# The output weights of a linear-attention block from sixteen 32-column products, and the work around them reordered

## The chip, the cores and the metric

The kernel runs on one core of a Trainium2 chip. The metric is the device time of one execution in microseconds (us). TensorE (PE) multiplies matrices, VectorE (DVE), ScalarE (ACT) and GpSimd (POOL) work on elements, and SyncE (SP) issues most of the transfers. PSUM, into which TensorE writes, has eight banks here called 0 to 7.

## The reference

For a sequence of 2048 rows of 448 elements, a linear-attention block with 16 heads of 28, and a gated feed-forward block; `phi` is positive, so the attention needs no softmax.

```python
def _A_ref(x, wqkv, wo):
    qkv = (x @ wqkv).reshape(B, S, 3, H, Dh).transpose(2, 0, 3, 1, 4)
    q, k, v = qkv[0], qkv[1], qkv[2]
    phi = lambda t: jnp.where(t > 0, t + 1, jnp.exp(t)) + 1e-6
    pq, pk = phi(q), phi(k)
    kv = jnp.einsum("bhsd,bhse->bhde", pk, v)
    z = jnp.einsum("bhsd->bhd", pk)
    num = jnp.einsum("bhqd,bhde->bhqe", pq, kv)
    den = jnp.einsum("bhqd,bhd->bhq", pq, z)[..., None] + 1e-6
    o = num / den
    return o.transpose(0, 2, 1, 3).reshape(B, S, D) @ wo
def _B_ref(x, w_gate, w_up, w_down):
    g, u = x @ w_gate, x @ w_up
    return (_gelu(g) * u) @ w_down
h = x + _A_ref(_layernorm(x), A_wqkv, A_wo)
h2 = h + _B_ref(_layernorm(h), B_w_gate, B_w_up, B_w_down)
```

## The kernel before, in words

**Tiles and stages.** The rows are cut into 16 tiles of 128, tiles into 8 pairs. First stage: each tile is normalised and transposed, `k_t` and `q_t` are its projections (four products of 448 columns each, L469), ScalarE and VectorE turn them into `pk` and `pq`, and the `pt` products (L488) sum pk against the normalised rows over all tiles in four PSUM banks (`BK_PT`, 4 to 7). Bank 7 also holds z in its upper half.

**The middle.** When the last `pt` product is done, `z1` (ScalarE) and `z0` (VectorE) bring z onto all partitions (`zbc`), and `evpD_3`, `evpA_0`, `evpA_1`, `evpD_2` copy the four banks to `pt_sb`. `kv` (L527, sixteen products of 112 columns) multiplies them with the v weights, and `kvm` masks the result into a block-diagonal `kvz`. The `w2` products (L547) multiply `kvz` with `wo`: the rows of the result, 448, are the rows of a folded output weight. Each of four groups writes one bank, and `evwA_0`, `evwD_1`, `evwA_2`, `evwD_3` copy them to `w2`. `dws0` and `dws1` are transfers that give `w2s`, a copy of w2 with its partition halves exchanged. Meanwhile the first pair of tiles gets its denominators: `t1` (pq times zbc, tile 0 on VectorE, others on GpSimd), `dr` (sum over a head), `deA` (plus epsilon, ScalarE), `rd` (reciprocal), `pn` (pq times rd, into `pqn`). `tro` (L599) transposes pqn on TensorE into banks 6 and 7, `evo` copies it out, and `out1` (L617) multiplies it with w2. Later pairs have the same steps in pair-wide form (`cqP`, `aqP`, `drP`, `deP`, `rdP`, `pnP`), a transposing transfer `oT`, and products on partition halves (`outA`, `outB`, L627 and L628). The q products that are left over fill TensorE's time between these.

**The feed-forward stage.** The normalised rows (`nh`, `wrap`, `hT`) are multiplied by gate and up weights in pairs of products that use one half of the rows of the array each (`gu2` for chunks of two tiles, `gu4` for chunks of four, L731 and L733). ScalarE's `ge` applies gelu to the gate's bank, VectorE's `hm` multiplies with the up bank into `hh`, each in two halves of 256 columns. `down` (L697, L678 for the last two tiles) sums over `hh`, `fo` adds the residual, `do` writes the tile. The last tile's columns are done in two pieces, so that the first piece's write overlaps the second's products.

**What sets the order.** Every operation is added to a graph, with buffers that it reads and writes, from which its waits follow. Which operation stands where on its engine is written out by hand: `ORDERS` lists the numbers of the operations for PE, ACT, DVE, POOL and SP. `HOLD` only says which of an operation's waits is issued first.

```python
self.order = {e: [self.all[int(i)] for i in o.split()] for e, o in zip(ENGS, orders)}
...
for w in sorted(keep, key=lambda w: (w[4] not in hold, -w[1])):
    slots.setdefault(w[2], []).append((w[0], w[1], w[4]))
```

## Time and profile before

| | |
|---|---|
| time, median of 3 runs | 190.62 us (190.51, 190.62, 191.12) |
| span of the profiled execution | 188.3 us |
| PE busy | 184.3 us (98%), 1813 matmuls |
| DVE busy | 129.3 us (69%) |
| ACT busy | 76.5 us (41%) |
| POOL busy | 50.0 us (27%) |

The span runs from the first to the last profiled instruction of one execution; that execution's own time is not listed apart from the three runs, of which the median lies 2.3 us above the span. Rows of a timeline give start, length, engine, line, operation, output and inputs, shape (for TensorE first the part of the array, rows by columns) and count. A row that merges several instructions ends when the last of them ends. Matmuls overlap: one of 448 columns is listed with some 0.35 us, while the next one may start after half of that.

### The profile page before, as it was taken

The numbers are of one execution on the slowest core, as the hardware profiler recorded it, in microseconds if no ns is written. First come the engines' busy times: TensorE is split into PE (matmuls) and PEld (weight loads), VectorE is DVE, ScalarE is ACT, GpSimd is POOL, SyncE is SP. The second block draws the span as 40 slices with busy tenths as digits, with TensorE's granted clock in tenths as the row PEclk, the third lists the DMA queues.
The fourth block names the chain that finished last, engine by engine and source line by source line (L and its number), as shares of the span: only waits on it lengthen the run. The fifth ranks groups of instructions, "written<-read, shape, count | busy, mean of one in ns | idle before, by whom it ended". The sixth has DMA issues, their size and how long they took to land.

```text
span 188.3 us, 4459 instructions
## 1 busy us (share of the span) xinstructions
PE 184.3 (98%) x1813; PEld 109.2 (58%) x1813; DVE 129.3 (69%) x330; ACT 76.5 (41%) x220; POOL 50.0 (27%) x91
## 2 busy tenths in 40 slices
PE   7999999999999999999999999999999999999994
PEld 7545555555688788965554555555545545454554
DVE  4999959999899998786796762562645244335432
ACT  3878752799963231432234222321242222224100
POOL 6067910704505686033614000206100000000000
PEclk9999999999999999999999999999999999999999
DMA  5996458999393526820005720000096000002024
GB/s 169 387 231 88 96 104 194 218 222 174 65 320 64 95 52 116 84 52 0 0 3 98 144 54 0 0 3 2 3 135 111 3 0 24 3 0 98 3 79 140
DMA packets 35076, 17.11 MB, mean 91 GB/s; under 512 B 26864, under 2 KB 33648, under 8 KB 35056
## 3 DMA queue, kind: packets, MB, share of 16 engines
q1 hardware_dynamic: 34432, 16.32, 41.1%
q10 hardware_dynamic: 624, 0.52, 0.8%
q8 instruction: 14, 0.23, 0.5%
q14 instruction: 6, 0.05, 0.1%
HBM read 8.26 MB, written 1.84 MB: 54 GB/s over the span
## 4 chain that ended last, share of the span: by engine, by line
PE 94%; DVE 3%; DMA 1%; issue 0%
PE ps L733 38%; PE ps L697 19%; PE ps L469 12%; PE ps L731 9%; PE ps L488 6%; PE ps L627 3%; PE ps L678 3%; PE ps L628 2%; DMA x_sb<-in_A_x_dram 1%; DVE st L413 1%; PE ps L617 1%; PE ps L547 1%; PE ps L527 1%; PE ps L443 0%; PE ps L654 0%; DVE den L572 0%
## 5 line engine op out<-in xcount | busy, mean ns | idle before, releaser
L733 PE MATMUL ps<-hnT,wgu_sb 64*128 64x512 bf16 (+1 forms) x490 | 88.8, 333 | 0.0
L731 PE MATMUL ps<-hnT,wgu_sb 64*128 64x512 bf16 (+1 forms) x490 | 88.6, 333 | 0.0
L751 ACT ACTIVATE gl<-ps 128x256 bf16<-128x256 f32 x112 | 36.6, 383 | 85.3 <-PE ps L731 84.4
L753 DVE TENSOR_TENSOR hh<-ps,gl 128x256 bf16<-128x256 f32 x112 | 42.1, 416 | 41.4 <-ACT gl L751 41.3
L733 PEld LDWEIGHTS ps<-hnT,wgu_sb 64*128 64x128 bf16 x490 | 45.2, 94 | 32.9 <-DVE hh L753 3.4
L731 PEld LDWEIGHTS ps<-hnT,wgu_sb 64*128 64x128 bf16 x490 | 45.4, 94 | 2.5
L697 PE MATMUL ps<-wd_sb,hh 64*128 64x448 bf16 x392 | 41.5, 349 | 0.0
L697 PEld LDWEIGHTS ps<-wd_sb,hh 64*128 64x128 bf16 x392 | 23.2, 94 | 14.5
L469 PE MATMUL ps<-wqk_sb,xnT 128*128 128x448 bf16 x128 | 27.4, 353 | 0.0
L413 DVE BATCH_NORM_STATS2 st<-x_sb 128x6 f32<-128x448 bf16 x32 | 19.2, 612 | 1.8 <-DMA x_sb<-in_A_x_dram 1.7
L585 POOL TENSOR_TENSOR t<-pq,zbc 128x448 f32<-128x448 bf16 x12 | 12.3, 1042 | 23.7 <-DVE pq L583 22.0
L469 PEld LDWEIGHTS ps<-wqk_sb,xnT 128*128 128x128 bf16 x128 | 11.9, 98 | 11.4 <-DVE pk L482 0.8
L488 PE MATMUL ps<-pk,xnn 128*128 128x448 bf16 x64 | 13.9, 352 | 0.0
L627 PE MATMUL ps<-w,pqnT 64*128 64x448 bf16 x49 | 11.5, 349 | 0.1
L425 POOL TENSOR_SCALAR ln<-mv 128x2 f32<-128x2 f32 x7 | 2.0, 291 | 35.2 <-DVE mv L414 35.0
L480 ACT ACTIVATE e<-ps 128x448 bf16<-128x448 f32 x16 | 8.5, 539 | 5.6 <-PE ps L469 5.5
L628 PE MATMUL ps<-pt_sb,pqnT 64*128 64x448 bf16 x42 | 10.2, 350 | 0.0
L633 DVE TENSOR_TENSOR x_sb<-ps,x_sb 128x448 bf16<-128x448 f32 x16 | 9.6, 616 | 0.7 <-PE ps L628 0.6
L662 POOL TENSOR_SCALAR hn<-x_sb,nm,rs 128x448 bf16<-128x448 bf16 x14 | 9.9, 719 | 0.4
L482 DVE SCALAR_TENSOR_TENSOR pk<-ps,e 128x448 bf16<-128x448 f32 x16 | 9.8, 617 | 0.1
L488 PEld LDWEIGHTS ps<-pk,xnn 128*128 128x128 bf16 x64 | 6.3, 98 | 5.9 <-DVE pk L482 0.3
L453 POOL TENSOR_SCALAR xnn<-x_sb,nm,rs 128x448 bf16<-128x448 bf16 x12 | 8.9, 744 | 2.2 <-ACT rs L422 1.9
(85 smaller groups left out, 160.5 us busy)
## 6 DMA issues: line engine op xcount, KB each, us to landing
out_dram<-x_sb SPq DMA_DIRECT2D x15, 112.0 KB, 1.8
wd_sb<-in_B_w_down_dram SPq DMA_DIRECT2D x1, 1568.0 KB, 8.4
x_sb<-in_A_x_dram SPq DMA_DIRECT2D x3, 448.0 KB, 5.9
wgu_sb<-in_B_w_gate_dram SPq DMA_DIRECT2D x1, 896.0 KB, 12.1
wgu_sb<-in_B_w_up_dram SPq DMA_DIRECT2D x1, 896.0 KB, 16.5
wgu_sb<-in_B_w_gate_dram SPq DMA_DIRECT2D x1, 672.0 KB, 6.1
wgu_sb<-in_B_w_up_dram SPq DMA_DIRECT2D x1, 672.0 KB, 8.5
wo_sb<-in_A_wo_dram SPq DMA_DIRECT2D x1, 392.0 KB, 7.5
```

Of the source, the lines that this page charges most:

```text
L413: op("dve", lambda e: e.bn_stats(st[:, t, :], src_ap), [b_src], [b_st[t]], "bnst%s_%d" % (tag, t))
L469: ins = e.matmul(ps[:, bk, 0:D], xnT[:, t, k, :], wqk_sb[:, k, c0:c0 + D], start=(k == 0), stop=(k == 3))
L488: ins = e.matmul(ps[:, BK_PT[c], 0:D], xnn[:, t % XN_R, c * 128:(c + 1) * 128], pk[:, ip, :], start=(t == 0), stop=(t == T - 1))
L585: op("pool", lambda e, n=n: e.tensor_tensor(t1[:, n, :], pq[:, a + n, :], zbc[:, :], ALU.mult), [b_pq[a + n]] + b_z, [b_t1[n]], "t1p_%d" % ...
L627: e.matmul(ps[:, BK_OUT[0], 0:D], pqnT[ra, i2, sg // 2, :], w2[ra, sg // 2, :], start=(sg == 0), stop=(sg == 5))
L628: ins = e.matmul(ps[:, BK_OUT[1], 0:D], pqnT[rb, i2, 3 + (sg + 1) // 2, :], (w2 if sg == 6 else w2s)[rb, sg // 2, :], start=(sg == 0), sto ...
L662: op("pool", lambda e, t=t, sh=sh: e.tensor_scalar(hn[:, sh, 0:D], x_sb[:, t, :], nm2[:, t:t + 1], rs2[:, t:t + 1], ALU.add, ALU.mult), [b ...
L697: ins = e.matmul(ps[:, bko[half][n], 0:D], hh[rows, j, sl[n]], wd_sb[rows, j, :], start=(j == 0 and (half == 0 or p == 6)), stop=(j == NJ ...
L731: first = e.matmul(psG[:, jj * N:(jj + 1) * N], wgu_sb[A_, k, j * 128:(j + 1) * 128], hnT[A_, ka_, c0:c0 + N], start=(k == 0), stop=(k == ...
L733: ins = e.matmul(psU[:, jj * N:(jj + 1) * N], wgu_sb[B_, k, j * 128:(j + 1) * 128], hnT[B_, kb_, c0:c0 + N], start=(k == 0), stop=(k == NK ...
L751: G.add("act", lambda e, gi=gi, cs_=cs_, psG=psG: e.activation(gl[:, gi, cs_], psG[:, cs_], AF.Gelu_apprx_tanh), r=[b_ps[BK_G[i]]], w=[b_g ...
L753: op("dve", lambda e, dst=dst, srcU=srcU, srcL=srcL: e.tensor_tensor(dst, srcU, srcL, ALU.mult), [b_ps[BK_U[i]], b_glh], [b_ar[j_][t % HR] ...
```

## The change

- The sum for `w2` is cut into blocks of 32 rows of the result: sixteen products with 32 columns of `kvz` each, which write 32 partitions of a bank; two blocks straddle two groups of heads and have two products each. `kvd`, a copy of 64 columns that gave the last group a full width, goes; the last 64 rows of w2's fourth piece are zeroed at the start instead (`w2pad`), and the exchanged copy `w2s` has a fourth piece, so that `dws1` carries 64x1792 instead of 64x1344 elements.
- The first pair's denominators and transposes (`a2_den(0)`) stand ahead of w2 in the graph, as they use banks that w2 then takes.
- The second pair (tiles 2 and 3) has its VectorE steps pair-wide, as the later pairs had already. `t1p_3` also waits for the first pair's pqn.
- Epsilon is a 29th column of `t1`, written once at the start; `deA` and `deP` go.
- All three full copies of the PT banks are ScalarE's (`evpA_0` to `evpA_2`).
- In the chunks of two tiles `ge` and `hm` work on 512 columns in one operation.
- The last tile's pieces are 320 and 128 columns instead of 224 and 224.
- `ORDERS` is new, and `HOLD` has an entry for most operations.

TensorE between the last `pt` products (L488, L560) and the first pair's output products (L617, L692); L469 and L541 are q products, L527 and L650 kv, L547 and L668 w2, L599 and L625 the transposes. Before:

```order
L488 MATMUL ps<-pk,xnn 128x448 x20
L469 MATMUL ps<-wqk_sb,xnT 128x448 x8
L527 MATMUL ps<-pt_sb,wv_sb 112x112 x16
L469 MATMUL ps<-wqk_sb,xnT 128x448 x8
L547 MATMUL ps<-wo_sb,hh 128x448 x6
L469 MATMUL ps<-wqk_sb,xnT 128x448 x4
L547 MATMUL ps<-wo_sb,hh 128x448
L599 MATMUL ps<-ident,pqn 128x128 x8
L469 MATMUL ps<-wqk_sb,xnT 128x448 x4
L617 MATMUL ps<-w,pqnT 128x448 x8
```

And now:

```order
L560 MATMUL ps<-pk,xnn 128x448 x20
L541 MATMUL ps<-wqk_sb,xnT 128x448 x12
L650 MATMUL ps<-pt_sb,wv_sb 112x112 x16
L625 MATMUL ps<-ident,pqn 128x128 x8
L541 MATMUL ps<-wqk_sb,xnT 128x448 x4
L668 MATMUL ps<-wo_sb,hh 32x448 x16
L541 MATMUL ps<-wqk_sb,xnT 128x448 x8
L692 MATMUL ps<-w,pqnT 128x448 x8
```

Three q tiles instead of two stand ahead of kv, the transposes moved from behind w2 to directly behind kv, and all of w2 stands together behind one more q tile.

ScalarE from z1 (L514, L637) to the copies of w2 (L551, L674); L519 and L642 are copies of PT banks, L574 the epsilon, L496/L497 and L568/L569 exponential and relu of q, L602 and L628 evo. Before:

```order
L514 ACTIVATE zbc<-ps 64x448
L519 ACTIVATE pt_sb<-ps 128x448 x2
L574 ACTIVATE den<-den,eps_d 128x16
L496 ACTIVATE eq<-ps 128x448 x2
L497 ACTIVATE pq<-ps 128x448
L574 ACTIVATE den<-den,eps_d 128x16 x2
L496 ACTIVATE eq<-ps 128x448
L497 ACTIVATE pq<-ps 128x448
L574 ACTIVATE den<-den,eps_d 128x16
L497 ACTIVATE pq<-ps 128x448
L551 ACTIVATE w<-ps 128x448 x2
```

And now:

```order
L637 ACTIVATE zbc<-ps 64x448
L642 ACTIVATE pt_sb<-ps 128x448 x2
L568 ACTIVATE eq<-ps 128x448
L642 ACTIVATE pt_sb<-ps 128x448
L568 ACTIVATE eq<-ps 128x448
L569 ACTIVATE pq<-ps 128x448 x2
L628 ACTIVATE pqnT<-ps 128x512 x2
L568 ACTIVATE eq<-ps 128x448
L569 ACTIVATE pq<-ps 128x448
L674 ACTIVATE w<-ps 128x448 x2
```

The third copy of a PT bank stands behind one exponential, and evo moved from behind w2's copies to ahead of them.

VectorE in the same place, from the copy of the fourth PT bank (L516, L639) on: L515 and L638 are z0, L569 and L597 t1, L572 and L600 dr, L575 and L602 rd, L576 and L603 pn, L531 and L654 kvm, L553 and L676 copies of w2; L609, L610, L613, L615 and L616 are cqP, aqP, drP, rdP and pnP. Before:

```order
L515 COPY zbc<-zbc 64x448
L565 TENSOR_TENSOR pq<-pq,eq 128x448
L569 TENSOR_TENSOR t<-pq,zbc 128x448
L572 TENSOR_REDUCE den<-t 128x16
L521 CAST pt_sb<-ps 128x448
L575 RECIPROCAL rd<-den 128x16
L572 TENSOR_REDUCE den<-t 128x16 x2
L531 TENSOR_TENSOR hh<-ps,mask 112x4x112
L575 RECIPROCAL rd<-den 128x16
L536 COPY hh<-hh 112x64
L572 TENSOR_REDUCE den<-t 128x16
L575 RECIPROCAL rd<-den 128x16
```

And now:

```order
L600 TENSOR_REDUCE den<-t 128x16
L602 RECIPROCAL rd<-den 128x16
L603 TENSOR_TENSOR pqn<-pq,rd 128x448 x2
L654 TENSOR_TENSOR hh<-ps,mask 112x4x112
L609 TENSOR_SCALAR eq<-eq 128x896
L613 TENSOR_REDUCE den<-t 128x32
L676 CAST w<-ps 128x448
L610 TENSOR_TENSOR pq<-pq,eq 128x896
L615 RECIPROCAL rd<-den 128x32
L676 CAST w<-ps 64x448
L616 TENSOR_TENSOR pqn<-pq,rd 128x896
```

Both pqn of the first pair now stand ahead of kvm, the copy of a PT bank is gone, and the second pair's wide steps stand among the copies of w2.

The diff, cut to what the steps speak of:

```diff
 ORDERS = (
...
-    " 190 157 203 216 169 181 232 182 248 194 195 207 220 208 236 252 221 237 253 238 222 294 257 260 301 297 299"
+    " 191 158 204 217 170 182 233 183 249 195 208 196 209 221 237 253 222 238 254 239 223 258 295 311 309 264 319"
...
 HOLD = {
-    66: (36,), 141: (140,), 165: (164,), 214: (213,), 216: (215,), 323: (302,), 326: (324,), 431: (340,), 704:
...
+    21: (20,), 33: (32,), 35: (34,), 36: (35,), 38: (35,), 42: (41,), 44: (43,), 45: (44,), 47: (44,),
...
-        t1 = sb("t1", [128, 2, D], F32)
+        t1 = sb("t1", [128, 2, H, DH + 1], F32)
...
-        w2s = pt_sb[:, 0:3, :]
+        w2s = pt_sb
...
+        op("dve", lambda e: e.memset(w2[B_, 3, :], 0.0), [], [b_w2t], "w2pad")
...
-        op("pool", lambda e: e.memset(eps_d[:], EPS), [], [b_epsd], "epsd")
+        op("pool", lambda e: e.memset(t1[:, :, :, DH:DH + 1], EPS), [], [b_epsd], "epsd")
...
-            if c in (0, 1):
+            if c in (0, 1, 2):
                 op("act", lambda e, c=c: e.activation(pt_sb[:, c, :], ps[:, BK_PT[c], 0:D], AF.Identity), [b_ps[BK_PT[c]]], [b_pt[c]], "evpA_%d" % c)
...
-        op("dve", lambda e: e.tensor_copy(kvz[:, 4 * D:4 * D + 64], kvz[:, 4 * D - 64:4 * D]), [b_kvm], [b_kvd], "kvd")
+        a2_den(0)
...
-        for c in range(4):
-            def fw2(e, c=c):
-                gs = (c, c + 1) if c < 3 else (3,)
-                ins = None
-                for g in gs:
-                    ins = e.matmul(ps[:, BK_W2[c], 0:D], kvc(g, c), wo_sb[:, g, :], start=(g == gs[0]), stop=(g == gs[-1]))
-                return ins
+        for c, parts in enumerate((((0, 0), (1, 0), (2, 0), (3, 0), (3, 1)), ((0, 1), (1, 1), (2, 1), (3, 2)), ((0, 2), (1, 2), (2, 2), (3, 3), (2, 3)), ((0, 3), (1, 3)))):
+            def fw2(e, c=c, parts=parts):
+                ins = None
+                for i, (q, g) in enumerate(parts):
+                    ins = e.matmul(ps[32 * q:32 * q + 32, BK_W2[c], 0:D], kvc(g, c, q), wo_sb[:, g, :],
+                                   start=q not in [x[0] for x in parts[:i]], stop=q not in [x[0] for x in parts[i + 1:]])
+                return ins
...
-            dma("sp", w2s[to, :, :], w2[of, 0:3, :], [b_w2s[h]], "dws%d" % h, r=b_w2[0:3], after=xts[-1:])
+            dma("sp", w2s[to, 0:3 + h, :], w2[of, 0:3 + h, :], [b_w2s[h]], "dws%d" % h, r=b_w2[0:3 + h], after=xts[-1:])
...
-            if p < 2:
+            if p < 1:
...
-                    op("act", lambda e, i=i: e.activation(den[:, i, :], den[:, i, :], AF.Identity, bias=eps_d[:, 0:1]), [b_den[i], b_epsd], [b_den[i]], "deA_%d" % t)
...
-            parts = [(BK_L[t][0], 0, D)] if t < T - 1 else [(BK_L[t][0], 0, D // 2), (BK_L[t][1], D // 2, D)]
+            parts = [(BK_L[t][0], 0, D)] if t < T - 1 else [(BK_L[t][0], 0, 320), (BK_L[t][1], 320, D)]
...
-                for hh_ in range(2):
-                    cs_ = slice(hh_ * 256, (hh_ + 1) * 256)
+                for hh_ in range(2 if nj == 1 else 1):
+                    cs_ = slice(hh_ * 256, (hh_ + 1) * 256) if nj == 1 else slice(0, 512)
```

102 lines of the change are left out of this document (53 added, 49 removed), and 135 rows, old and new, of tables (HOLD, ORDERS).

## The prediction

> **What bounds the kernel now.** I read the page's busy rows and slices first, then the waits of TensorE, then the timelines of the middle (27 to 52 us) and of the end.
>
> ```profile
> span 188.3 us, 4459 instructions
> ...
> PE 184.3 (98%) x1813; PEld 109.2 (58%) x1813; DVE 129.3 (69%) x330; ACT 76.5 (41%) x220; POOL 50.0 (27%) x91
> ...
> PEclk9999999999999999999999999999999999999999
> ```
>
> TensorE (PE) is busy for 98% of the span at the full clock. Ends of matmuls are modelled, so that alone does not prove that it never waits; the list of its waits does more:
>
> ```profile
> PE ps L407 <- POOL eps_d L383: 1.0, 1, 1.0
> PE ps L443 <- DVE xnn L435: 0.4, 1, 0.4
> ```
>
> Both belong to the first six microseconds, which the change leaves alone. A short wait can still hide under a modelled end, so I also read intervals between starts. This is TensorE in the middle (start, length, line, shape, count):
>
> ```profile
> 30.45 3.95 PE L488 MATMUL ps<-pk,xnn 128*128 128x448 bf16 x20
> 34.23 1.68 PE L469 MATMUL ps<-wqk_sb,xnT 128*128 128x448 bf16 x8
> 35.96 1.03 PE L527 MATMUL ps<-pt_sb,wv_sb 128*112 128x112 bf16 x16
> 36.83 1.68 PE L469 MATMUL ps<-wqk_sb,xnT 128*128 128x448 bf16 x8
> 38.34 1.30 PE L547 MATMUL ps<-wo_sb,hh 112*128 112x448 bf16 x6
> 39.48 0.92 PE L469 MATMUL ps<-wqk_sb,xnT 128*128 128x448 bf16 x4
> 40.24 0.35 PE L547 MATMUL ps<-wo_sb,hh 112*128 112x448 bf16 x1
> 40.43 0.61 PE L599 MATMUL ps<-ident,pqn 128*128 128x128 bf16 x8
> ```
>
> From 30.45 to 34.23 twenty 448-column matmuls start: 0.189 us each. Eight from 36.83 to 38.34 give 0.189 again. But the eight from 34.23 should end at 34.23 + 8 x 0.189 = 35.74, and the kv products (L527) start at 35.96: a wait of 0.22. The chain of waits says for what:
>
> ```profile
> 35.38 0.54 DVE pt_sb L521
> ...
> 35.96 1.03 PE ps L527 x16
> ...
> 40.59 0.45 PE ps L599 x8
> ```
>
> It is evpD_2, VectorE's copy of one of the PT banks. Elsewhere the kernel is a stream of matmuls at their own rate. So a gain has to come from fewer matmul intervals, from this 0.22, or from the end after the last matmul. What VectorE (DVE), ScalarE (ACT) or GpSimd (POOL) save is worth nothing unless TensorE waited for it.
>
> **The change part by part.**
>
> *kv's wait.* Twelve q products now stand ahead of kv in place of eight: kv is due at 34.23 + 12 x 0.189 = 36.50. The three copies of the PT banks go to ScalarE, with eq_5 between the second and the third.
>
> ```profile
> 34.43 0.98 ACT L519 ACTIVATE pt_sb<-ps 128x448 bf16<-128x448 f32 x2 [1.16 <-PE ps L488]
> ...
> 35.62 0.96 ACT L496 ACTIVATE eq<-ps 128x448 bf16<-128x448 f32 x2
> ...
> 40.88 1.08 ACT L602 ACTIVATE pqnT<-ps 128x512 bf16<-128x512 bf16 x2
> ```
>
> Two such operations take 0.96 to 0.98 together, so the next one starts some 0.43 after one. The third copy is the fourth operation from 34.43: it starts at 35.72 and ends 0.54 later, at 36.26, which is 0.24 ahead of 36.50. The wait goes: **-0.22**. If ScalarE slips by more than 0.24, kv waits again for the excess.
>
> *The output weights.* Before, seven products (six and one) take seven intervals: 1.32. Now there are sixteen products of 32 columns, each onto 32 partitions; products on different quarters of the array may run together, those on the same quarter not. The order is w2_3, w2_0, w2_1, w2_2, and the quarters in that order are 0 1, 0 1 2 3 3, 0 1 2 3, 0 1 2 3 2. Issued in order, with a quarter taken up again when it is free, that fills five intervals: (0 1) (0 1 2 3) (3 0 1 2) (3 0 1 2) (3 2), or 5 x 0.189 = 0.95. No product of a quarter of the columns stands in this trace. The nearest rows are products that use half of the rows each:
>
> ```profile
> 48.30 0.33 PE L654 MATMUL ps<-ident,hn 128*128 128x128 bf16 x3
> 48.57 0.36 PE L627 MATMUL ps<-w,pqnT 64*128 64x448 bf16 x1
> 48.57 0.36 PE L628 MATMUL ps<-pt_sb,pqnT 64*128 64x448 bf16 x1
> ...
> 180.08 0.35 PE L697 MATMUL ps<-wd_sb,hh 64*128 64x448 bf16 x1
> 180.36 0.36 PE L678 MATMUL ps<-wd_sb,hh 128*128 128x448 bf16 x1
> ```
>
> Two halves start at the same 48.57 and have the length of one. I take quarters of the columns to do likewise. The same rows show the price of going between array layouts: transposes take 0.45 / 8 = 0.056 each (the chain's L599), so the three from 48.30 should give way at 48.47, and the halves start at 48.57: 0.10 late. On the way back, 180.08 to 180.36 is 0.28 in place of 0.19: 0.09 late. The sixteen products stand together, between q products, so there is one switch each way: 0.19. Sum: 0.95 + 0.19 - 1.32 = **-0.18**. Bounds: five intervals without a price for the switches, -0.37; sixteen intervals one behind another, 3.02 + 0.19 - 1.32 = +1.89. I take the value near the first, because the nearest rows overlap fully.
>
> [...]
>
> *What could come late behind it.* The first pair's transposes (tro) now follow kv directly, at 36.50 + 0.87 = 37.37 (kv's length of 35.96 to 36.83 without its wait). They need pqn from VectorE:
>
> ```profile
> 33.37 0.39 DVE L515 COPY zbc<-zbc 64x448 f32<-64x448 f32 x1
> ...
> 34.10 0.62 DVE L569 TENSOR_TENSOR t<-pq,zbc 128x448 f32<-128x448 bf16 x1
> 34.76 0.62 DVE L572 TENSOR_REDUCE den<-t 128x16 f32<-128x448 f32 x1
> ...
> 35.82 0.24 DVE L575 RECIPROCAL rd<-den 128x16 f32<-128x16 f32 x1
> ...
> 37.19 0.61 DVE L531 TENSOR_TENSOR hh<-ps,mask 112x448 bf16<-112x448 f32 x1
> ...
> 38.62 0.56 DVE L576 TENSOR_TENSOR pqn<-pq,rd 128x448 bf16<-128x448 bf16 x1
> ...
> 40.63 0.62 DVE L553 CAST w<-ps 128x448 bf16<-128x448 f32 x1
> ...
> 42.24 0.62 DVE L583 TENSOR_TENSOR pq<-pq,eq 128x896 bf16<-128x896 bf16 x1
> ...
> 45.16 1.05 DVE L586 TENSOR_REDUCE den<-t 128x32 f32<-128x896 f32 x1
> ```
> ```profile
> 34.27 3.39 POOL L569 TENSOR_TENSOR t<-pq,zbc 128x448 f32<-128x448 bf16 x3 [8.83 <-DVE pq L565]
> ```
>
> z0 ends at 33.76 as before. Tile 0's product then ends at about 34.4, its reduction at 35.05, its reciprocal at 35.3. GpSimd's product of tile 1 starts at 33.85 and takes 3.39 / 3 = 1.13 to 1.3: 35.15. Reduction 0.62, reciprocal 0.24, two pqn of 0.56: 36.6 for tile 1, 37.1 for tile 0, against a need at 37.37 and, four transposes later, 37.59. It holds by 0.5. The q product behind tro ends its issue at 37.37 + 0.45 + 0.76 = 38.58; kvm, after kv, is done at 37.54 + 0.61 = 38.15. So w2 starts at 38.67. Its last group, w2_2, writes a bank that evo_1 empties: tro's result at 38.0, two ScalarE operations in 1.08, 39.1; the group's turn is 38.67 + 3 x 0.189 = 39.24. It holds, by 0.1: the narrowest place. out1 is due at 38.67 + 0.95 + 0.10 + 8 x 0.189 = 41.23 and reads its last weight piece three intervals later, 41.80. VectorE gets there through kvm (38.15), cqP_2 and the pair-wide reduction (some 0.4 and 1.05; GpSimd's product of tile 3, which now waits for pqn, is ready at 37.1 + 1.13 = 38.3), evwD_1 from 39.6 (0.62), aqP_2 (0.62), rdP_1 (0.3) and evwD_3 (0.62): 41.8 by whole lengths. Successive operations overlap (the chain counts 0.54 for evpD_2 where a copy of this size is 0.62 long), so five steps save 0.4: it holds by some 0.3. I cost all of these at nothing; a slip beyond the margin costs its excess.
>
> *The end.* The last tile's second piece has 128 columns in place of 224; the matmul time is that of the same 448 columns.
>
> ```profile
> 184.56 0.39 DVE L682 TENSOR_TENSOR x_sb<-ps,x_sb 128x224 bf16<-128x224 f32 x1 [0.72 <-PE ps L678]
> 184.98 1.67 SPq L683 DMA_DIRECT2D out_dram<-x_sb  x2
> 185.90 0.39 DVE L682 TENSOR_TENSOR x_sb<-ps,x_sb 128x224 bf16<-128x224 f32 x1 [0.95 <-PE ps L678]
> ```
> ```profile
> out_dram<-x_sb SPq DMA_DIRECT2D x15, 112.0 KB, 1.8
> ...
> out_dram<-x_sb SPq DMA_DIRECT2D x2, 56.0 KB, 1.6
> ```
>
> A 448-column add takes 0.62 (L553's width), a 224-column one 0.39: some 0.001 per column, so 128 columns take 0.29, 0.10 less. The write shrinks from 56 to 32 KB: between 112 and 56 KB the rows differ by 0.2, so 0.09 less by that slope, nothing if the rest is a fixed cost; I take 0.04. The first piece's write is issued earlier than the second add ends (its 320-column add starts 14 x 0.056 = 0.78 before the second, at 185.12, and ends at 185.6; an issue takes some 0.45). **-0.14**, with bounds -0.10 and -0.19.
>
> *What is hidden.* The epsilon becomes a 29th column of what is reduced: the ScalarE additions go (ten short operations), the reductions read 4% more. kvd goes. The second pair's steps are pair-wide. For the first two gate/up chunks ScalarE and VectorE work on 512 columns in one operation; by
>
> ```profile
> L753 DVE TENSOR_TENSOR hh<-ps,gl 128x256 bf16<-128x256 f32 x112 | 42.1, 416 | 41.4 <-ACT gl L751 41.3
> ```
>
> two cost 0.83 now and one wide one about 0.68. All of it runs under TensorE's matmuls and buys nothing; its danger is that a bank comes free later, as the first half's result no longer goes ahead. A gate/up group of 14 pairs lasts 1.5, and its bank is needed again one group later; one wide ScalarE operation (0.6) and one wide VectorE operation (0.68) take 1.3 of it. That cover is thin whenever another VectorE operation stands between. GpSimd's product now writes rows that lie 29 apart; the nearest row is L569's 1.13 for the same elements, which I take; a quarter more (0.3) on tile 1 would still leave the transposes 0.2.
>
> **Sum.** -0.22 - 0.18 - 0.14 = -0.54 on a span of 188.3. The three runs shown give 190.51, 190.62 and 191.12; the median lies 2.3 above the span, and I carry that unchanged: 190.62 - 0.54 = **190.08**. About 0.3% (0.57 us) is what a measurement of this kernel can tell from no change, so the forecast lies right at that line.
>
> **The rivals.**
>
> A: *the quarters don't run together.* Each 32-column product then takes a whole interval: -0.22 + 1.89 - 0.14 = +1.53, **192.15**, slower. It decides at w2: by the sum above the change is worth nothing at eight intervals for the sixteen products, and slower by 0.3% at eleven. For it: nothing in this trace is tiled by columns, and the four quarters would read four moving streams at once. Against it: the row halves start together. Chance 0.14.
>
> B: *they run two at a time*, as the halves do. In order that makes eight intervals, 1.51 + 0.19 - 1.32 = +0.38 and in all +0.02: **190.64**, no change. For it: the trace shows two at once and never four. [...] Chance 0.10.
>
> C: *a new wait takes the old one's place*: w2_2 for evo_1, out1 for evwD_3, or gate/up for a wide hm. Margins of 0.1 to 0.25 against operations of 0.6: one slipped operation costs 0.3 to 0.5, **190.5**. A repeated one in the fourteen wide groups would cost more. Chance 0.10.
>
> **How the numbers follow.** Forecast 0.66, A 0.14, B 0.10, C 0.10. The forecast's own spread is -0.3 to -0.9 (switches free, larger saving at the end); some six tenths of it lie beyond -0.57. Faster: 0.66 x 0.63 = 0.42. Slower: A and a little of C, 0.17. Within: 0.41. The range reaches down to -0.9 with 0.1 for the runs' scatter, 189.6, and up over B and C to 190.9; A stays outside.
>
> **What would show it.** Right: in the timeline the sixteen L668 products start in groups of up to four within some 0.02 and take about 1.0 from first start to the next q product, plus 0.1 at either side; kv starts 0.189 behind the last q product; the last add takes 0.29. Wrong: L668 starts 0.19 apart one by one (A), in twos (B); a hole ahead of L668's last group, of out1 (L692) or between gate/up groups (C).

## The result, and the profile after

| | median us | lowest to highest | runs |
|---|---|---|---|
| before | 190.55 | 190.29 to 191.12 | 18 |
| after | 191.07 | 190.71 to 191.75 | 18 |

The ratio is 1.0027 with an interval of 1.0017 to 1.0037. The kernel became slower by about 0.5 us; the forecast was 190.08, its range 189.6 to 190.9.

The page after says little by itself: TensorE is still busy for 98% of a span that is 0.9 longer.

```profile
span 189.2 us, 4434 instructions
PE 185.0 (98%) x1822; PEld 131.5 (70%) x1822; DVE 130.6 (69%) x310; ACT 73.6 (39%) x197; POOL 52.8 (28%) x91
```

TensorE's timeline after, through the middle and at the start of the last stage (start, length, line, shape, count, and in brackets a wait and what ended it):

```profile
34.76 2.43 PE L541 MATMUL ps<-wqk_sb,xnT 128*128 128x448 bf16 x12
37.03 0.99 PE L650 MATMUL ps<-pt_sb,wv_sb 128*112 128x112 bf16 x16
37.85 0.61 PE L625 MATMUL ps<-ident,pqn 128*128 128x128 bf16 x8
38.30 0.92 PE L541 MATMUL ps<-wqk_sb,xnT 128*128 128x448 bf16 x4
39.15 1.05 PE L668 MATMUL ps<-wo_sb,hh 112*32 112x448 bf16 x16
40.13 1.69 PE L541 MATMUL ps<-wqk_sb,xnT 128*128 128x448 bf16 x8
41.65 0.73 PE L692 MATMUL ps<-w,pqnT 128*128 128x448 bf16 x3
42.88 1.12 PE L692 MATMUL ps<-w,pqnT 128*128 128x448 bf16 x5 [0.50 <-DVE w L676]
43.84 4.79 PE L541 MATMUL ps<-wqk_sb,xnT 128*128 128x448 bf16 x24
48.54 0.95 PE L729 MATMUL ps<-ident,hn 128*128 128x128 bf16 x14
...
181.42 0.93 PE L753 MATMUL ps<-wd_sb,hh 128*128 128x448 bf16 x4
```

Three things are to be read here. The kv products (L650) start at 34.76 + 12 x 0.189 = 37.03, without a wait. The sixteen products of w2 (L668) take 40.13 - 39.15 = 0.98 up to the next q product. And the first pair's output products (L692, out1) start with three, then have a hole: 41.65 + 3 x 0.189 = 42.22, but the fourth starts at 42.88, **0.66 late**. The list of TensorE's waits, which before had only two entries of the first microseconds, names it:

```profile
PE ps L692 <- DVE w L676: 0.5, 1, 0.5
```

L676 is VectorE's copy of w2's last piece, evwD_3. VectorE's and GpSimd's timelines after show why it came late:

```profile
38.05 0.62 DVE L654 TENSOR_TENSOR hh<-ps,mask 112x448 bf16<-112x448 f32 x1
38.59 0.38 DVE L609 TENSOR_SCALAR eq<-eq 128x896 bf16<-128x896 bf16 x1
39.91 1.12 DVE L613 TENSOR_REDUCE den<-t 128x32 f32<-128x928 f32 x1 [0.93 <-POOL t L612]
40.95 0.61 DVE L676 CAST w<-ps 128x448 bf16<-128x448 f32 x1
41.48 0.61 DVE L610 TENSOR_TENSOR pq<-pq,eq 128x896 bf16<-128x896 bf16 x1
42.01 0.34 DVE L615 RECIPROCAL rd<-den 128x32 f32<-128x32 f32 x1
42.27 0.55 DVE L676 CAST w<-ps 64x448 bf16<-64x448 f32 x1
...
42.75 1.41 DVE L616 TENSOR_TENSOR pqn<-pq,rd 128x896 bf16<-128x896 bf16 x1
```
```profile
35.81 1.04 POOL L612 TENSOR_TENSOR t<-pq,zbc 128x448 f32<-128x448 bf16 x1
38.08 1.80 POOL L612 TENSOR_TENSOR t<-pq,zbc 128x448 f32<-128x448 bf16 x1 [1.23 <-DVE pqn L603]
42.17 2.88 POOL L612 TENSOR_TENSOR t<-pq,zbc 128x448 f32<-128x448 bf16 x2 [2.29 <-DVE pq L610]
```

GpSimd's product of tile 3 (t1p_3, at 38.08) took 1.80, where the same operation for tile 2 took 1.04. The pair-wide reduction drP_1 (L613) waited 0.93 for it. Everything behind drP_1 on VectorE's queue moved with it: evwD_3 ended at 42.82, and out1 wanted it at 42.22.

**Where the time went.** I cut the span at two starts that the change leaves comparable: the q products ahead of kv (L469 and L541) and the first 448-column product of the last stage (L678 and L753).

| | before | after |
|---|---|---|
| first statistics of tile 4 to the q products ahead of kv | 26.21 | 26.38 |
| from there to the last stage | 146.13 | 146.66 |
| from there to the end of the span (188.26 and 189.15 with two places) | 7.90 | 7.73 |

The first line starts at VectorE's statistics of tile 4 because that operation waits for a transfer that lands at another time in each run; this is chance, not the change:

```profile
8.02 0.62 DVE L413 BATCH_NORM_STATS2 st<-x_sb 128x6 f32<-128x448 bf16 x1
```
```profile
8.38 0.63 DVE L485 BATCH_NORM_STATS2 st<-x_sb 128x6 f32<-128x448 bf16 x1 [0.26 <-DMA x_sb<-in_A_x_dram]
```

The first row is before, the second after; in the other runs it stood between 7.94 and 8.71, without order by kernel. Without this 0.36 the change is +0.17 + 0.53 - 0.17 = +0.53, the 0.52 that the medians show.

The end became shorter as expected. VectorE's last two adds after:

```profile
186.18 0.49 DVE L757 TENSOR_TENSOR x_sb<-ps,x_sb 128x320 bf16<-128x320 f32 x1 [1.28 <-PE ps L753]
186.96 0.29 DVE L757 TENSOR_TENSOR x_sb<-ps,x_sb 128x128 bf16<-128x128 f32 x1 [0.29 <-PE ps L753]
```

The middle is the question: kv's wait gone and w2 shorter should give about -0.47, and it shows +0.53. Out1's wait is 0.66 of that difference. The rest is in intervals between starts: 0.07 ahead of a q product at 47.69, 0.09 at the transposes of the next stage (48.54), 0.10 at the first gate/up product (51.10), 0.14 inside a later gate/up group (76.86).

### The profile page after: what moved, and what is told of

Same layout as the page of the kernel before. It is cut to its first block, busy times and chain, and to the rows that moved or that the text cites. A ratio compares the mean times of both kernels' runs of the same rounds, so it can differ in the third digit from the quotient of the medians.

```text
span 189.2 us, 4434 instructions
## 1 busy us (share of the span) xinstructions
PE 185.0 (98%) x1822; PEld 131.5 (70%) x1822; DVE 130.6 (69%) x310; ACT 73.6 (39%) x197; POOL 52.8 (28%) x91
## 4 chain that ended last, share of the span: by engine, by line
PE 88%; DVE 5%; DMA 3%; POOL 1%; SPq 1%; issue 0%
PE ps L808 28%; PE ps L772 19%; PE ps L806 18%; PE ps L541 9%; PE ps L560 6%; DMA x_sb<-in_A_x_dram 3%; PE ps L702 3%; PE ps L753 3%; PE ps L703 2%; POOL t L612 1%; DVE den L600 1%; SPq L417 1%; DVE pqn L603 1%; DVE st L485 1%; PE ps L692 1%; DVE den L613 1%
## 5 line engine op out<-in xcount | busy, mean ns | idle before, releaser
L826 ACT ACTIVATE gl<-ps 128x256 bf16<-128x256 f32 (+1 forms) x98 | 35.6, 413 | 87.9 <-PE ps L806 87.9
L828 DVE TENSOR_TENSOR hh<-ps,gl 128x256 bf16<-128x256 f32 (+1 forms) x98 | 41.1, 455 | 41.1 <-ACT gl L826 40.7
L772 PE MATMUL ps<-wd_sb,hh 64*128 64x448 bf16 x392 | 40.9, 349 | 0.0
L772 PEld LDWEIGHTS ps<-wd_sb,hh 64*128 64x128 bf16 x392 | 28.5, 94 | 9.0
L541 PE MATMUL ps<-wqk_sb,xnT 128*128 128x448 bf16 x128 | 27.4, 354 | 0.1
L541 PEld LDWEIGHTS ps<-wqk_sb,xnT 128*128 128x128 bf16 x128 | 12.1, 99 | 11.9 <-DVE pk L554 1.3
L612 POOL TENSOR_TENSOR t<-pq,zbc 128x448 f32<-128x448 bf16 x14 | 16.8, 1216 | 11.7 <-DVE pq L610 10.5
L560 PE MATMUL ps<-pk,xnn 128*128 128x448 bf16 x64 | 13.9, 353 | 0.0
L497 POOL TENSOR_SCALAR ln<-mv 128x2 f32<-128x2 f32 x7 | 1.9, 266 | 40.0 <-DVE mv L486 39.8
L703 PE MATMUL ps<-pt_sb,pqnT 64*128 64x448 bf16 x49 | 11.5, 349 | 0.0
L560 PEld LDWEIGHTS ps<-pk,xnn 128*128 128x128 bf16 x64 | 6.2, 98 | 6.0 <-DVE pk L554 0.7
L489 POOL TENSOR_SCALAR nm<-mv 128x1 f32<-128x1 f32 (+1 forms) x19 | 5.1, 269 | 17.7 <-DVE mv L486 17.4
```

What stands on the lines that cost most here:

```text
L541: ins = e.matmul(ps[:, bk, 0:D], xnT[:, t, k, :], wqk_sb[:, k, c0:c0 + D], start=(k == 0), stop=(k == 3))
L560: ins = e.matmul(ps[:, BK_PT[c], 0:D], xnn[:, t % XN_R, c * 128:(c + 1) * 128], pk[:, ip, :], start=(t == 0), stop=(t == T - 1))
L612: op("pool", lambda e, n=n: e.tensor_tensor(t1[:, n, :, 0:DH], pq[:, a + n, :].rearrange("p (h d) -> p h d", h=H), zbc[:, :].rearrange("p ...
L703: ins = e.matmul(ps[:, BK_OUT[1], 0:D], pqnT[rb, i2, 3 + (sg + 1) // 2, :], w2s[rb, sg // 2, :], start=(sg == 0), stop=(sg == 5))
L772: ins = e.matmul(ps[:, bko[half][n], 0:D], hh[rows, j, sl[n]], wd_sb[rows, j, :], start=(j == 0 and (half == 0 or p == 6)), stop=(j == NJ ...
L826: G.add("act", lambda e, gi=gi, cs_=cs_, psG=psG: e.activation(gl[:, gi, cs_], psG[:, cs_], AF.Gelu_apprx_tanh), r=[b_ps[BK_G[i]]], w=b_gl ...
```

## The experiments

The theory at that point: TensorE's savings are real, and out1's wait, caused by t1p_3 being held up while VectorE's cqP_2 runs, takes them back. The main rivals: the wait that the change gave t1p_3 (for both pqn of the first pair) is the cause; the copies of w2 simply stand too late in VectorE's order; w2's sixteen products gain nothing. "Middle" below is the second line of the table above, read in each run's timeline. It was 146.13 in e8_before_again and 146.68 in e7_after_again, so a single reading of it is good to a few hundredths there. The ratio is not the quotient of the two medians; the two differ by up to 0.001 (e9: 1.0008 and 1.0016).

| run | median us | before beside it | ratio, interval | middle |
|---|---|---|---|---|
| e1_cq2_behind_reduction | 190.52 | 190.46 | 1.0001, 0.9990 to 1.0013 | 146.21 |
| e2_w2_copies_first | 191.50 | 190.46 | 1.0053, 1.0039 to 1.0066 | 147.22 |
| e3_no_wait_for_pqn | 190.86 | 190.46 | 1.0021, 1.0009 to 1.0032 | 146.57 |
| e4_full_width_w2 | 191.64 | 190.46 | 1.0069, 1.0051 to 1.0086 | 147.46 |
| e5_fast_steps_apart | 190.33 | 190.48 | 0.9998, 0.9989 to 1.0008 | 146.03 |
| e6_fast_steps_apart_full_w2 | 190.43 | 190.48 | 0.9999, 0.9989 to 1.0008 | 146.05 |
| e7_after_again | 190.93 | 190.48 | 1.0028, 1.0014 to 1.0041 | 146.68 |
| e8_before_again, one run | 190.34 | 190.48 | none | 146.13 |
| e9_small_waits_removed | 190.84 | 190.54 | 1.0008, 0.9994 to 1.0022 | 146.49 |
| e10_small_waits_removed_full_w2 | 190.55 | 190.54 | 0.9993, 0.9977 to 1.0010 | 146.88 |
| e11_q14_and_pk7_only | 190.36 | 190.64 | 0.9984, 0.9971 to 0.9997 | 146.03 |
| e12_small_waits_and_first_hm | 190.75 | 190.64 | 1.0012, 1.0003 to 1.0021 | 146.31 |

e7 and e8 are the two kernels unchanged. Their records:

> The kernel after, unchanged, on the chip of the fifth and sixth experiments. The first stage's offset of 0.53 against the kernel before: if it is the arrival of x's third transfer (the first statistics of tile 4 started at 8.02 before and at 8.38 after), it varies from run to run: 8.0 to 8.7 here too. The wait of out1, 0.66, is there again whatever the first stage does. Time 0.5 above the kernel before.

> The kernel before, unchanged, for a second profile of it: if the arrival of x's third transfer varies, the first statistics of tile 4 start at another time than 8.02 (8.0 to 8.7), with the span moving along by 0.3 or more; kv's wait of 0.2 behind the last q product is there again.

In e7 the same operation took 1.79 and the same wait stood at out1 with 0.66, so neither was chance.

**e1_cq2_behind_reduction.** Only cqP_2 (number 370) moves, from ahead of the reduction drP_1 (348) to behind it:

```diff
-    " 308 305 296 370 348 316 371 349 320 350 325 328 326 329 327 330 374 339 335 375 340 336 376 395 396 342 355"
+    " 308 305 296 348 370 316 371 349 320 350 325 328 326 329 327 330 374 339 335 375 340 336 376 395 396 342 355"
```

> The kernel after, with one VectorE operation moved: the fast SBUF-to-SBUF step cqP_2 (0.38 us) stands behind the pair-wide reduction drP_1 instead of ahead of it, so that it does not run beside GpSimd's product t1p_3. Theory 1 (the loss is the 0.66 us wait of out1 for evwD_3, and it starts with t1p_3 being slowed from 1.04 to 1.80 us by cqP_2): t1p_3 takes 1.04 to 1.1, drP_1 starts some 0.7 earlier, out1's wait falls below 0.1, and the time falls by 0.5 to 0.6 against the kernel after, to about 190.5. Theory 2 (t1p_3 is slow for another reason, or the chain through t1p_3's wait for pqn is simply too long): t1p_3 stays at 1.6 or more, out1's wait stays at 0.5 or more, time within 0.15 of the kernel after. Theory 3 (the loss is the 0.53 us of the first stage and the later waits, and TensorE gives a gain in the middle back): out1's wait goes, but the time falls by less than 0.2.

GpSimd's and VectorE's timelines of e1:

```profile
38.56 1.04 POOL L612 TENSOR_TENSOR t<-pq,zbc 128x448 f32<-128x448 bf16 x1 [1.23 <-DVE pqn L603]
```
```profile
39.63 1.12 DVE L613 TENSOR_REDUCE den<-t 128x32 f32<-128x928 f32 x1 [0.48 <-POOL t L612]
40.67 0.38 DVE L609 TENSOR_SCALAR eq<-eq 128x896 bf16<-128x896 bf16 x1
```

t1p_3 is back at 1.04, and out1's wait falls from 0.66 to 0.21 (below 0.1 was expected). The time falls by some 0.5 against after (1.0001 against 1.0027). So the place of one 0.38 VectorE operation was worth all of the loss against before: this part of the theory is shown. But the kernel is now only as fast as before, not faster by the 0.5 that TensorE saved: a second part was still unexplained.

**e2_w2_copies_first.** Both copies of w2 (316 and 320) move ahead of drP_1:

```diff
-    " 308 305 296 370 348 316 371 349 320 350 325 328 326 329 327 330 374 339 335 375 340 336 376 395 396 342 355"
+    " 308 305 296 370 316 320 348 371 349 350 325 328 326 329 327 330 374 339 335 375 340 336 376 395 396 342 355"
```

> The kernel after, with VectorE's two copies of w2 (evwD_1, evwD_3) ahead of the pair-wide reduction drP_1. Theory 1 and 2 alike: out1 no longer waits for evwD_3 whatever t1p_3 does (t1p_3 still 1.6 to 1.8 us), time 0.5 to 0.65 below the kernel after, about 190.45. Theory 3: time falls by less than 0.2, as later waits (the first pair-wide pqn arrives later, so its transposing transfer and the first outA) take the gain.

A miss: it became slower still. Out1's wait was gone, but another came. VectorE, ScalarE and TensorE in e2:

```profile
40.13 1.15 DVE L676 CAST w<-ps 128x448 bf16<-128x448 f32 x2 [0.98 <-PE ps L668]
...
43.14 1.77 DVE L616 TENSOR_TENSOR pqn<-pq,rd 128x896 bf16<-128x896 bf16 x1
```
```profile
47.14 0.48 ACT L492 ACTIVATE ln<-mv,eps_t 128x1 f32<-128x1 f32 x2 [1.43 <-DVE mv L486]
```
```profile
48.44 0.93 PE L541 MATMUL ps<-wqk_sb,xnT 128*128 128x448 bf16 x4 [1.14 <-ACT eq L568]
```

The copies are behind w2's products, so VectorE idled 0.98 for them and did drP_1, pnP_1, the residual adds (hr) and the statistics later. ScalarE waited 1.43 for the statistics with an exponential queued behind, which frees the bank of the last q tile (q_14); and TensorE waited 1.3 for that bank. This is what the first theory had left out: behind out1 it is VectorE's chain that TensorE meets, not only one late copy.

**e3_no_wait_for_pqn.** The added wait of t1p_3 is taken out:

```diff
-[b_pq[a + n]] + b_z + (b_pqn[0] if a + n == 3 else []), [b_t1[n]], "t1p_%d" % (a + n))
+[b_pq[a + n]] + b_z, [b_t1[n]], "t1p_%d" % (a + n))
```

> The kernel after, with t1p_3's added wait for the first pair's pqn taken away; t1p_3 may then run beside pn_1 and pn_0. Theory 1 (GpSimd's product and VectorE's SBUF-to-SBUF steps slow each other): t1p_3 starts at about 36.9 instead of 38.1 and takes 1.8 or more, the two pn go from 0.62 to 0.8 or more, the transposes wait for pqn by 0.2 to 0.6, while out1's wait shrinks by as much or more; time within 0.3 of the kernel after. Theory 2 (the chain is too long because of this wait, no contention): t1p_3 takes 1.04 and ends 1.9 earlier, pn stay at 0.62, out1's wait is gone, time 0.6 below the kernel after.

TensorE's and VectorE's timelines of e3:

```profile
37.98 0.93 PE L625 MATMUL ps<-ident,pqn 128*128 128x128 bf16 x8 [0.37 <-DVE pqn L603]
```
```profile
36.43 2.02 DVE L603 TENSOR_TENSOR pqn<-pq,rd 128x448 bf16<-128x448 bf16 x2
```

t1p_3 now starts at 36.40 and takes its 1.04, but the two pqn beside it take 2.02 in place of after's 1.16, and the transposes wait for them instead. The added wait was a protection of pqn, not a fault. The rival falls: it buys 0.1 to 0.2 of the 0.5.

**e4_full_width_w2.** e2 with the seven full-width products of before (the zeroed pad of kvz longer, so that the last group has its full width):

```diff
-                for i, (q, g) in enumerate(parts):
-                    ins = e.matmul(ps[32 * q:32 * q + 32, BK_W2[c], 0:D], kvc(g, c, q), wo_sb[:, g, :],
...
+                for g in gs:
+                    o = g * D + c * 128 if c < 3 else 4 * D - 64
+                    ins = e.matmul(ps[:, BK_W2[c], 0:D], kvz[:, o:o + 128], wo_sb[:, g, :], start=(g == gs[0]), stop=(g == gs[-1]))
```

> The kernel of the second experiment (copies of w2 first), with w2 from seven full-width products again instead of sixteen 32-column ones (64 further columns of kvz are zeroed at the start for it). Theory 1: w2's stretch from the end of the q product to the start of the next grows from about 1.07 to 1.32, no waits there, so the time is 0.25 above the second experiment. Rival: the quarters' products save nothing on balance (their switches, or out1 waits that were hidden): within 0.1 of the second experiment.

It is 0.14 slower than e2 in the median and 0.24 longer in the middle, though both wait 1.3 at q_14. The intervals of the two ratios overlap, so the times don't price w2. The traces show where the 0.24 went: in this order VectorE's copies stand waiting for w2, and they waited 1.23 in place of e2's 0.98.

```profile
40.39 1.15 DVE L677 CAST w<-ps 128x448 bf16<-128x448 f32 x2 [1.23 <-PE ps L670]
```

VectorE's copies of hn ended 0.24 later with it. Here w2's length reaches the end by way of VectorE's chain.

**e5_fast_steps_apart.** No fast VectorE step stands beside a GpSimd product in the middle any more: the order is drP_1, both copies of w2, rdP_1, pnP_1, and then cqP_2 and aqP_2 (370, 371). In a later gate/up group a wide multiply (hmW0_9, 480) goes ahead of the copy wrap_6 (415), which there stood beside a GpSimd product and took 1.10 in place of 0.26:

```diff
-    " 308 305 296 370 348 316 371 349 320 350 325 328 326 329 327 330 374 339 335 375 340 336 376 395 396 342 355"
+    " 308 305 296 348 316 320 349 350 370 371 325 328 326 329 327 330 374 339 335 375 340 336 376 395 396 342 355"
...
-    " 451 499 500 408 405 452 409 390 453 406 410 407 474 503 477 393 418 415 504 480 505 483 610 486 460 457 489"
+    " 451 499 500 408 405 452 409 390 453 406 410 407 474 503 477 393 418 480 415 504 505 483 610 486 460 457 489"
```

> The kernel after, with VectorE's order changed in two places so that its fast SBUF-to-SBUF steps keep out of GpSimd's products and out of the way of what TensorE waits for. In the middle: kvm, drP_1, both copies of w2, rdP_1, pnP_1, and only then cqP_2 and aqP_2 (so t1p_4 and t1p_5 start behind pnP_1). At 75 us: hmW0_9 ahead of wrap_6, which ran beside t1p_13. Theory (VectorE's chain through the middle, lengthened by steps that run beside GpSimd's, is what took the gain): t1p_3 1.04, pnP_1 1.09 instead of 1.41, t1p_5 1.04 instead of 1.88, wrap_6 0.26 instead of 1.10; out1's wait and the three small ones ahead of gate/up (0.07, 0.09, 0.10) go, and the one at 76.9 (0.14) goes: 0.9 to 1.05 below the kernel after, 190.0 to 190.15, 0.2 to 0.3% below the kernel before. Rival (as in the second experiment, something queued behind gets late: the exponential that frees the last q tile's bank, or the second pair's transposing transfer): a wait of 0.3 or more ahead of the last q tiles or of the first outA, time 190.4 or more.

GpSimd's products of e5, and pnP_1 on VectorE:

```profile
37.60 1.04 POOL L612 TENSOR_TENSOR t<-pq,zbc 128x448 f32<-128x448 bf16 x1 [1.23 <-DVE pqn L603]
43.27 2.04 POOL L612 TENSOR_TENSOR t<-pq,zbc 128x448 f32<-128x448 bf16 x2 [4.63 <-DVE pq L610]
```
```profile
41.14 1.09 DVE L616 TENSOR_TENSOR pqn<-pq,rd 128x896 bf16<-128x896 bf16 x1
```

Every product of GpSimd behind tile 1's (1.48) is at 1.02 to 1.05, pnP_1 at 1.09 (after 1.41), out1 and the gate/up group wait for nothing. Still both expectations were missed: the theory's 190.0 to 190.15 and the rival's wait of 0.3 or more with 190.4. The middle is 0.63 shorter than after's and 0.10 shorter than before's. What is left are a wait of 0.26 at q_14, 0.09 at the transposes L729 and 0.09 at the first gate/up product. Of the 0.47 that TensorE saves here, 0.10 shows; the rest was still missing.

**e6_fast_steps_apart_full_w2.** e5 with e4's seven products:

> The fifth experiment's kernel with w2 from seven full-width products (64 further columns of kvz zeroed at the start). If VectorE's chain no longer sets the middle: 0.25 above the fifth, as w2's stretch is 1.32 instead of 1.07. If it still does: within 0.1 of the fifth.

```profile
38.92 1.49 PE L670 MATMUL ps<-wo_sb,hh 112*128 112x448 bf16 x7
40.25 1.68 PE L541 MATMUL ps<-wqk_sb,xnT 128*128 128x448 bf16 x8
```

TensorE works 0.25 longer on w2 (0.094 + 0.979 = 1.07 against 1.32), and the middle is the same: 146.05 against 146.03. The wait at q_14 went from 0.26 to 0.04 in exchange. So in this version w2's saving is real on TensorE and worth nothing in the time: something else sets the end of the stretch. VectorE doesn't wait for w2 in this order, as it does in e2 and e4.

**e9 to e12: the small waits by order alone.** e9 moves four things in e5: ScalarE's exponential eq_10 (268) ahead of ln2_0 (331), so that q_14's bank no longer waits for the statistics; the reciprocal rdP_2 (375) behind the copies wr64 (340, 336); the copy evhD_1 (342) ahead of cqP_3 and aqP_3 (395, 396); and cq_0 (297) behind the copy pk_7 (145) in the first stage.

```diff
-    " 218 234 250 289 292 294 240 293 224 241 225 310 312 259 260 318 314 257 256 263 265 266 262 272 271 269 331"
-    " 333 334 332 268 275 283 277 284 280 338 274 278 281 343 421 424 427 430 433 436 439 476 473 479 482 485 488"
+    " 218 234 250 289 292 294 240 293 224 241 225 310 312 259 260 318 314 257 256 263 265 266 262 272 271 269 268"
+    " 331 333 334 332 275 283 277 284 280 338 274 278 281 343 421 424 427 430 433 436 439 476 473 479 482 485 488"
...
-    " 136 171 87 172 88 159 197 184 102 160 185 103 226 117 198 118 227 132 242 210 211 133 297 156 157 144 145"
+    " 136 171 87 172 88 159 197 184 102 160 185 103 226 117 198 118 227 132 242 210 211 133 156 157 144 145 297"
...
-    " 308 305 296 348 316 320 349 350 370 371 325 328 326 329 327 330 374 339 335 375 340 336 376 395 396 342 355"
+    " 308 305 296 348 316 320 349 350 370 371 325 328 326 329 327 330 374 339 335 340 336 375 376 342 395 396 355"
```

> The kernel of e5_fast_steps_apart with the four waits that its trace still shows on TensorE taken away by order alone: q_14 0.26 (eq_10 now ahead of ln2_0 on ScalarE), trh 0.09 (rdP_2 behind wr64_0 on VectorE), gu2_0 0.09 (evhD_1 ahead of cqP_3 and aqP_3), pk_7 0.10 (cq_0 behind pk_7's copy). Theory (the change's gain is real and what is lost again are small waits, one for one): 0.53 below e5, that is 190.33 - 0.53 = 189.8 where the kernel before gives 190.48, a ratio of 0.996 to 0.997. Rival (VectorE's chain through hr and the statistics sets the end of this stretch, so that a wait removed in one place comes back at the next): within 0.15 of e5, ratio 0.999 to 1.000, and the waits show up at q_14 or at out1 again.

VectorE's and TensorE's timelines of e9 at the third pair's output products:

```profile
52.67 1.12 DVE L613 TENSOR_REDUCE den<-t 128x32 f32<-128x928 f32 x1 [0.43 <-POOL t L612]
53.71 0.68 DVE L828 TENSOR_TENSOR hh<-ps,gl 128x512 bf16<-128x512 f32 x1
```
```profile
53.94 0.35 PE L702 MATMUL ps<-w,pqnT 64*128 64x448 bf16 x1 [0.55 <-DVE den L613]
```

The theory failed: by the ratios e9 is 0.2 slower than e5, not 0.5 faster. It is the rival's picture, though the waits came at other places than it named: q_14 and the first gate/up product no longer wait, the transposes L729 wait 0.20, and 0.71 comes back at 53.94. The row puts that down to the reduction, which those products don't read; what they do need is the third pair's pqn through a DMA transpose, which was issued at 49.06 and took 4.7 to land, until 53.76.

e10 is e9 with seven products for w2:

> The kernel of e9_small_waits_removed with w2 as the seven full-width products of the kernel before. It prices the sixteen products without a wait behind them. Theory (sixteen products hold TensorE 0.25 less than seven): 0.25 above e9. Rival (VectorE's chain sets the end here, whatever w2 costs): within 0.1 of e9.

Its median is 0.3 below e9's, against the theory and outside the rival's 0.1 too, with intervals that overlap. Its profiled run was the slowest of its twelve (191.18), so that its middle of 146.88 isn't typical. In it the same transpose landed in 3.0 and nothing waited for it, but gate/up groups waited for VectorE's multiplies (0.35 and 0.40 at two of them). I take from e10 only that it shows no cost of seven products here either.

e11 keeps only e9's moves of eq_10 and cq_0, so that nothing goes later on VectorE; e12 adds to e9 the multiply hmW0_0 (422) ahead of the reduction drP_3 (399):

```diff
-    " 356 358 399 422 357 359 425 400 360 401 428 606 447 431 380 383 368 434 448 365 437 384 381 440 385 607 382"
+    " 356 358 422 399 357 359 425 400 360 401 428 606 447 431 380 383 368 434 448 365 437 384 381 440 385 607 382"
```

> The kernel of e5_fast_steps_apart with two of the four moves of e9_small_waits_removed only: eq_10 ahead of ln2_0 on ScalarE, cq_0 behind pk_7's copy; rdP_2 and evhD_1 stay where e5 has them, so that nothing goes later on VectorE. Theory (TensorE's gain is real, and e9 lost it because evhD_1 ahead of cqP_3 made GpSimd's t1p_6, drP_3 and hmW0_0 late): q_14's 0.26 and pk_7's 0.10 go, trh waits about 0.25 in place of 0.09, gu2_0 0.09 as before, no wait at outA_2: 0.1 to 0.2 below e5, a ratio of 0.999. Rival (VectorE's chain sets the end of this stretch): what is won at q_14 is waited for at trh one for one, 0.1 below e5 at most, ratio 0.9995 to 1.000.

> The kernel of e9_small_waits_removed with one more move on VectorE: hmW0_0, the first gate/up group's multiply, ahead of the reduction drP_3, which waited 0.43 for GpSimd there. Theory: hmW0_0 ends near 53.5 in place of 54.39, gu2_2 no longer waits for its bank, and of e9's waits only trh's 0.20 is left, with the landing of the third transpose (oT_2: 2.9 in e5, 4.7 in e9) as chance may have it: 0.3 to 0.4 below e9, ratio 0.998 to 0.999. Rival (VectorE has no room left in this stretch): another group of gate/up waits instead, gu2_3 or outA_3, because drP_3 and hmW0_1 behind it come later; within 0.1 of e9.

In e12 the multiply ended at 53.42 instead of 54.39, as meant, and TensorE waited for the DMA transpose itself, which landed after 4.6:

```profile
53.62 0.35 PE L702 MATMUL ps<-w,pqnT 64*128 64x448 bf16 x1 [0.37 <-DMA pqnT<-pqn]
```

The hole there is 0.53. The theory fails again, in the rival's way, at another place than the rival named.

e11 shows the bound most plainly. TensorE and VectorE in e11:

```profile
42.86 4.70 PE L541 MATMUL ps<-wqk_sb,xnT 128*128 128x448 bf16 x24
47.76 0.95 PE L729 MATMUL ps<-ident,hn 128*128 128x128 bf16 x14 [0.20 <-DVE hn L722]
```
```profile
47.51 0.20 DVE L722 COPY hn<-hn 128x64 bf16<-128x64 bf16 x2
```

The twenty-four q products now run without a hole. They end their issue at 42.86 + 24 x 0.189 = 47.40, and the transposes start 0.36 later, when VectorE has put their operand in place (47.71). The 0.26 that went at q_14 came back here one for one; the middle is 146.03, as in e5. With 0.9984 e11 is the only version whose interval lies below 1; it is one of eleven such intervals, and its median of 190.36 is no lower than e5's 190.33. The stages of e11 and e5, without the chance at tile 4, sum to 0.17 and 0.15 less than before, as much as the tail saves. I would not call it more than 0.1 to 0.2%.

**What set the end.** The same two places before (VectorE's copies of hn, TensorE's transposes of hn):

```profile
47.06 0.20 DVE L647 COPY hn<-hn 128x64 bf16<-128x64 bf16 x2
```
```profile
47.69 0.94 PE L654 MATMUL ps<-ident,hn 128*128 128x128 bf16 x14
```

VectorE was ready at 47.26 and TensorE came at 47.69: a margin of **0.43**, for a saving of 0.47 on TensorE. After, from z0 to the same copies:

```profile
33.90 0.39 DVE L638 COPY zbc<-zbc 64x448 f32<-64x448 f32 x1
48.29 0.20 DVE L722 COPY hn<-hn 128x64 bf16<-128x64 bf16 x2
```

VectorE's own chain from z0 to there, 13.89 before (from 33.37), is 14.59 after (from 33.90 to 48.49) and 14.11 in e11 (from 33.60), and drP_1's wait for GpSimd's t1p_3 is in it: 0.93 in after, 0.48 in e1, e5 and e11. So the saving could at most have shown 0.43 up to there, and with VectorE 0.2 to 0.7 longer it could show little or none.

All the traces bear this out. In after and in every experiment on it but e3 (where TensorE comes 0.20 behind) the transposes of hn start 0.05 to 0.08 after VectorE's last copy of hn, whatever w2 took. In e1, e5, e6 and e11 VectorE's chain is 14.11 to 14.13, and the transposes come 13.31 to 13.33 behind the start of the q products ahead of kv, with sixteen products for w2 or with seven; before it was 13.46. In after the copies ended at 48.49 and the transposes started at 48.54: without out1's hole, and with VectorE's chain as it was, they could have come hardly earlier. So out1's wait is not the loss by itself. The delay of drP_1 is, and it reached TensorE at out1 and again at the transposes; e1 makes it smaller at both places; e2 takes away the wait at out1 alone and makes VectorE's chain 15.16.

## Why the prediction was wrong

- *kv's wait, -0.22*: right. kv starts 0.189 behind the last q product, as "What would show it" asked.
- *The output weights, -0.18*: right in kind, small by 0.07. The sixteen products took 0.98, the switch ahead of them 0.094; the switch behind is part of the 0.98. That is 1.07 against 1.32. That 0.98 lies near the five intervals of the prediction (0.95) is luck. In the trace after four products start at 39.15 to 39.17, four at 39.35 to 39.37, three at 39.54 to 39.55 and three at 39.73 to 39.74, with one late at 39.64 and one at 39.84. Each quarter has four of the sixteen, so this looks like four intervals, each quarter going through its own four without waiting for its place in the whole order (the trace doesn't name the quarter), and 0.10 of lateness. Rivals A and B fall: sixteen intervals would be 3.02, eight 1.51. Against sixteen products one behind another the four quarters come to 3.02 / 0.98 = 3.1, with the lateness and the switch behind in it.
- *The end, -0.14*: right, -0.17.
- *evo_1's margin of 0.1*: it did not quite hold. evo_1 is the second of the two in the row below, and ended at 39.58. The late product of w2 started at 39.64, where by its quarter's pace it would have at 39.54 to 39.55, and the profile puts 0.2 of idle time among w2's weight loads down to evo. By the order of five intervals the last group's turn was 39.15 + 3 x 0.189 = 39.72, which held; the quarters ran ahead of that and met evo_1. It cost an estimated 0.10 inside the 0.98.

```profile
38.50 1.08 ACT L628 ACTIVATE pqnT<-ps 128x512 bf16<-128x512 bf16 x2 [0.38 <-PE ps L625]
```

- *What could come late behind it, "I cost all of these at nothing"*: **the step that failed**. It named the right place, out1's wait for evwD_3, and the right chain. The term that was mis-sized is GpSimd's product of tile 3. I took 1.13 from a row in which nothing fast ran beside it, and had it "ready at 38.3", which is 38.83 in the trace after, where the stretch begins 0.53 later. It took 1.80 and ended at 39.88, 1.05 late: 0.67 by its length, the rest because it started late, at 38.08. The pqn that it waits for ended at 38.00 where the prediction has 37.1 + 0.53 = 37.63. The late start ate most of the margin of "some 0.3", and the length made a wait of 0.66 of it: 0.67 earlier, evwD_3 would have ended at an estimated 42.15, still ahead of 42.22. The smaller waits (0.07, 0.09, 0.10, 0.14, and 0.10 in the first stage, at a `pt` product at 24.15) are other places where TensorE met VectorE's chain; the sum had none of them.
- The step had a second fault, which e2, e5, e6 and e11 showed: the list ended at out1. Behind it VectorE's chain runs on to the transposes of the next stage, with a margin of 0.43, and the change makes that chain longer. The sentence that VectorE's time "is worth nothing unless TensorE waited for it" is true of savings; it doesn't say how much of TensorE's saving there is room for.
- *Rival C*, a new wait in the place of the old one, is what happened, at all three of its places (w2_2 for evo_1 by an estimated 0.10, out1 for evwD_3, and a wide gate/up multiply by 0.14). Its price of 0.3 to 0.5 was one slip; there were several, and its chance of 0.10 was too low for margins of 0.1 to 0.3 at the end of chains of several durations.

What stays open: 0.07 of the first stage's +0.17 that I could not put to a wait, and how much of e11's 0.9984 is real. No run brought VectorE's chain below the 13.89 of before (the shortest, 13.94 to 13.97, are those of e9, e10 and e12, with rdP_2 behind the copies), and none filled the 0.48 that VectorE stands idle ahead of drP_1. That TensorE's saving would then show in the time is argued, not shown.

## What to carry to other kernels

Where one engine is busy 98% of the time, a saving on it ahead of a meeting point is worth at most the margin by which the next engine's chain arrives there, unless that chain gets shorter too: write those margins down (here 0.43 at the transposes of hn) before adding up what the first engine saves. Price an operation of GpSimd by what VectorE will be running beside it in the new order (here 1.04 or 1.80), not by a row in which VectorE ran something else. When waits that are removed one by one come back at the next meeting point with the same size, reordering has given what it can: it is the other engine's work that has to shrink (which no run here tried).
